# Early phase of a transformer block kernel recorded in the order in which its transfers are needed

## The chip, the cores and the metric

The kernel runs on one core of a Trainium2 chip. The metric is device time in microseconds (us) of one execution. 2% is the mark for calling one kernel faster than another. Engines: PE multiplies matrices, PEld is its weight loads, DVE and ACT work on vectors, POOL and SP in the early phase mostly issue transfers. A number such as L379 is a line of the kernel's source.

## The reference

```python
def reference(A_x, A_wqkv, A_wo, B_x, B_w_gate, B_w_up, B_w_down):   # x: 2048 x 1024, bf16
    h  = x + attention(layernorm(x) @ wqkv) @ wo     # 32 heads of 32; each position looks at
                                                     # 8 positions, 2 apart, itself and before
    n  = layernorm(h)
    return h + ((n @ w_gate) * (n @ w_up)) @ w_down  # F = 3584
```

(The attention is cut to a comment; B_x is not used.)

## The kernel before

The 2048 rows are cut into four chunks of 512. PE works through chunk after chunk; all other engines are to stay out of its way. Work of DVE and ACT that is not tied to a matmul is written as generators, from which a "background" draws pieces while the groups of matmuls are recorded: every group of PE (8 matmuls, 1.73 us) earns credit, every piece spends some. So it is the recording that fixes the order of each engine's instructions.

The projections to q, k and v are six blocks of weights (0 and 1 are q, 2 and 3 are k, 4 and 5 are v), each block four groups of eight matmuls. q, k and v go through memory, to turn the layout from features on partitions to (head, place) on partitions, and DVE does attention from there.

```python
def ln1(c):                                   # first normalization of chunk c, in the background
    xts = load_x(c, "x", nc.gpsimd)
    yield "later", 8.0 if c < 3 else 5.0
    ...
    def norm(t):
        ln = normalize(xts[t], mv4, rs4, t)
        nc.sync.dma_start_transpose(lnTs[c][:, :, bass.ts(t, 128)], ln[:])

load_x0(0); load_x0(1); load_w(2)             # first loads, in order, on the SP queue:
load_x0(2); load_w(2);  load_x0(3)            # x, x, block 0, x, block 1, x
...
def qkv(c, blocks, last=False):
    for b in blocks:
        for j in range(4):
            ps = psum.tile([128, TC], F32, tag="mm", ...)   # one of 8 banks
            mm_group(ps, wts["qkv", b], j, lnTs[c])         # PE: 8 matmuls
            evac_qkv(c, b * 4 + j, ps)                      # ACT copies, SP stores to memory
            bg.step(GROUP_US)
...
qkv(0, range(1, 6))          # all of q, k, v of chunk 0 (block 0's q is done in the start)
bg.add(ln1(3))
start_attention(0)           # loads q, k, v of chunk 0 through POOL, then DVE works
qkv(1, range(6))
start_attention(1)
qkv(2, range(6))
...
```

## Time and profile before

| kernel before | us |
|---|---|
| median of 3 runs | 813.73 (812.7 to 814.17) |
| span in the profile | 812.0 |
| PE busy | 795.3 |
| first matmul of full width (512 columns) | 20.23 |
| first product of attention on DVE | 67.82 |
| first matmul of the first output projection | 165.27 |
| first matmul of the last output projection | 491.47, after a wait of 4.88 |

The page's first two parts, for the kernel before. A row of the second part gives the busy tenths of an engine in 40 equal slices of the span, here 20.3 us each; PEclk is the granted clock of PE in tenths.

```profile
span 812.0 us, 9901 instructions
PE 795.3 (98%) x3700; PEld 410.6 (51%) x3769; DVE 551.8 (68%) x580; ACT 254.9 (31%) x562; POOL 171.8 (21%) x172
...
PE   7999999999999999999999997999999999999998
...
PEclk9999999999999999999999998999999999999999
```

PE is the bound: the row has three slices that are not full, the first, the 25th (near 490 us) and the last. The clock row has its one dent in the same 25th slice: there PE does not only stand, part of what it does afterwards runs at a lower clock (0.51 from 491.4 to 497.3 us). This wait of PE is thus paid twice, once as idle time and once as slow matmuls that look busy.

### The profile page before, as it was taken

Reading aid. Unit: us, or ns where it says so; the run is one execution under the profiler, and the core shown is the slowest. Engines: PE = TensorE matmul, PEld = TensorE weight load, DVE = VectorE, ACT = ScalarE, POOL = GpSimd, SP = SyncE. Lnnn points to the kernel's source line nnn. Section 1 sums busy time; section 2 is a strip of 40 time slices with the busy share of each in tenths; the row PEclk is TensorE's granted clock in tenths of the full one; section 3 lists DMA queues with packets and bytes.
Section 4 is the critical chain, followed back from the end, with each engine's and each line's share of the span. In section 5 each row is a group of like instructions: output and inputs, shape, how many; then the busy total and the mean of one; then the engine's idle time right before and its main releaser. Section 6 shows DMA issues by size and latency. Waiting matters only on the chain.

```text
span 812.0 us, 9901 instructions
## 1 busy us (share of the span) xinstructions
PE 795.3 (98%) x3700; PEld 410.6 (51%) x3769; DVE 551.8 (68%) x580; ACT 254.9 (31%) x562; POOL 171.8 (21%) x172
## 2 busy tenths in 40 slices
PE   7999999999999999999999997999999999999998
PEld 5444444444444444444444443466666666644445
DVE  4538999999899898999989945635646565311111
ACT  2554444314333310023333100245545555400000
POOL 3100000200001000002000001497878778100000
PEclk9999999999999999999999998999999999999999
DMA  9999564999855948848564596533323233465600
GB/s 310 317 254 235 123 192 105 260 281 253 289 161 189 316 117 277 281 132 288 182 199 145 136 312 141 129 99 84 103 54 104 55 102 90 152 219 182 187 27 27
DMA packets 194448, 144.32 MB, mean 178 GB/s; under 512 B 83424, under 2 KB 188000, under 8 KB 192352
## 3 DMA queue, kind: packets, MB, share of 16 engines
q1 hardware_dynamic: 189856, 118.51, 52.5%
q0 software_dynamic: 4544, 25.17, 8.9%
q8 instruction: 30, 0.49, 0.3%
q14 instruction: 18, 0.15, 0.1%
HBM read 114.29 MB, written 22.02 MB: 168 GB/s over the span
## 4 chain that ended last, share of the span: by engine, by line
PE 83%; issue 13%; DMA 3%; SPq 0%; POOL 0%; DVE 0%; ACT 0%; POOLq 0%
PE ps L343 19%; PE acc L524 18%; PE pg L343 7%; PE pu L343 7%; PE pz L575 6%; PE py L575 6%; PE px L575 6%; PE wo L466 5%; PE pv L575 3%; PE accl L514 3%; DMA od<-oD 1%; DMA x<-in_A_x_dram 1%; DMA oT<-od 1%; POOL oT L443 0%; SPq L226 0%
## 5 line engine op out<-in xcount | busy, mean ns | idle before, releaser
L343 PE MATMUL ps<-lnT,w_qkv 128*128 128x512 bf16 x721 | 158.4, 379 | 0.8
L343 PEld LDWEIGHTS <-w_qkv 128*128 128x128 bf16 x736 | 72.0, 98 | 86.6
L343 PE MATMUL pg<-lnT,w_wg 128*128 128x512 bf16 x439 | 105.0, 379 | 0.5
L343 PE MATMUL pu<-lnT,w_wu 128*128 128x512 bf16 x439 | 104.9, 379 | 0.4
L524 PE MATMUL acc<-w_wd,gs 128*128 128x512 bf16 x439 | 96.7, 379 | 0.5
L262 ACT CAST sg<-ps 128x512 bf16<-128x512 f32 x96 | 55.5, 586 | 65.3 <-PE ps L343 59.0
L506 DVE TENSOR_TENSOR h<-acc,h 128x512 bf16<-128x512 f32 x28 | 17.4, 682 | 81.8 <-PE acc L524 81.8
L428 DVE TENSOR_TENSOR pv<-vD,at 128x4096 bf16<-128x4096 bf16 x32 | 72.4, 2287 | 0.4
L388 DVE TENSOR_TENSOR prod<-qD,kD 128x4096 bf16<-128x4096 bf16 x32 | 72.3, 2285 | 0.0
L524 PEld LDWEIGHTS <-gs 128*128 128x128 bf16 x448 | 43.9, 98 | 52.8
L343 PEld LDWEIGHTS <-w_wg 128*128 128x128 bf16 x448 | 43.8, 98 | 52.9
L343 PEld LDWEIGHTS <-w_wu 128*128 128x128 bf16 x448 | 43.8, 98 | 52.9
L466 PE MATMUL wo<-w_wo,oT 128*128 128x512 bf16 x251 | 58.4, 392 | 5.1 <-DMA oT<-od 4.9
L491 ACT CAST gs<-pg 128x512 bf16<-128x512 f32 x56 | 32.8, 586 | 91.5 <-PE pg L343 88.1
L440 POOL DMA_DIRECT2D od<-oD x4 | 2.2, 544 | 251.0 <-DVE oD L438 153.5
L575 PE MATMUL px<-lnT,w_pair 128*128 128x512 bf16 x210 | 52.5, 380 | 0.9
L496 ACT CAST us<-pu 128x512 bf16<-128x512 f32 x56 | 32.8, 586 | 60.1 <-PE pu L343 54.4
L551 POOL TENSOR_TENSOR sw<-w_pair 128x512 fp32r<-128x512 bf16 x28 | 36.5, 1302 | 60.5 <-issue 32.2
L466 PEld LDWEIGHTS <-oT 128*128 128x128 bf16 x256 | 25.7, 101 | 37.4 <-DMA oT<-od 5.4
L178 ACT ACTIVATE rs<-mv,eps 128x1 f32<-128x1 f32 x32 | 9.4, 294 | 104.6 <-DVE mv L175 99.7
L553 POOL TENSOR_TENSOR sw<-w_pair 128x512 fp32r<-128x512 bf16 x28 | 36.9, 1318 | 0.0
L390 DVE TENSOR_TENSOR prod<-prod 128x4096 bf16<-128x4096 bf16 x16 | 36.6, 2289 | 0.3
(128 smaller groups left out, 1066.1 us busy)
## 6 DMA issues: line engine op xcount, KB each, us to landing
w_wd<-in_B_w_down_dram SPq DMA_DIRECT2D x32, 896.0 KB, 6.2
w_wg<-in_B_w_gate_dram SPq DMA_DIRECT2D x14, 1024.0 KB, 8.1
w_wu<-in_B_w_up_dram SPq DMA_DIRECT2D x14, 1024.0 KB, 6.0
w_wo<-in_A_wo_dram SPq DMA_DIRECT2D x8, 1024.0 KB, 6.9
w_pair<-in_B_w_gate_dram SPq DMA_DIRECT2D x14, 512.0 KB, 4.0
w_pair<-in_B_w_up_dram SPq DMA_DIRECT2D x14, 512.0 KB, 5.4
kd<-sg SPq DMA_DIRECT2D x32, 144.0 KB, 3.3
vd<-sg SPq DMA_DIRECT2D x32, 144.0 KB, 2.7
```

The lines of the kernel that those rows point to most:

```text
L262: nc.scalar.copy(sg[:, HB:HB + TC], ps[:])
L343: nc.tensor.matmul(ps[:], lhsT=wt[:, ko, bass.ts(j, 128)], rhs=rhs[:, ko, :], start=(ko == 0), stop=(ko == KO - 1))
L388: nc.vector.tensor_tensor(prod[:, j], qD[:], kD[:, :, o:o + SUB], ALU.mult)
L390: nc.vector.tensor_tensor(prod[:, :, 0:16], prod[:, :, 0:16], prod[:, :, 16:32], ALU.add)
L428: nc.vector.tensor_tensor(pv[:, j], vD[:, :, o:o + SUB], at[:, w, None, :].to_broadcast((128, DH, SUB)), ALU.mult)
L466: nc.tensor.matmul(ps[:], lhsT=oTs[c][:, kk, t, :], rhs=wts["wo", c, hf][:, kk, :], start=(kk == 0), stop=(kk == KO - 1))
L491: nc.scalar.copy(gs[:], pg[:])
L496: nc.scalar.copy(us[:], pu[:])
L524: nc.tensor.matmul(acc[t][:], lhsT=hT[f][:, bass.ts(t, 128)], rhs=wts["wd", c, hf, b][:, j, :], start=(f == 0), stop=(f == NF - 1))
L551: nc.gpsimd.tensor_tensor(sw[:, 0], a21, a22, ALU.add)
L553: nc.gpsimd.tensor_tensor(sw[:, 2], a11, a21, ALU.subtract)
L575: nc.tensor.matmul(ps[:], lhsT=lhs[:, ko, :], rhs=rhs[:, ko, :], start=(fresh and ko == 0), stop=(ko == 3), skip_group_check=not fresh)
```

## The change

The change records the early work in the order in which its data is needed. q and k of chunk 0 are followed by q and k of chunk 1, and only then by the two chunks' v; so attention, which begins with q and k, can begin sooner. The transposes of the "second normalization" (that of chunk 2) are held until the first q and k loads are out. And x's last tile of chunk 0 stands ahead of the second weight block, which waits for it. The first transposes now lie in two banks each. The x of chunks 1 to 3 is now loaded through SP's queue instead of POOL's, and the weights of later blocks are held back. The core of the diff (cut: the class that splits the normalization into statistics, normalization and transposes, the limits of `pump`, which loads the next weights, the wait for v, and renamings; the comments are mine):

```diff
     load_x0(0)
     load_x0(1)
-    load_w(2)
+    load_w0(0, 4)               # block 0 in two halves
     load_x0(2)
-    load_w(2)                   # block 1 in two halves
+    load_w0(4, 4)
     load_x0(3)
...
-        pts[t] = psum.tile([128, KO, 128], BF, tag="mm", name=f"pt{t}")
+        for hf in range(2):     # first transposes in two banks, so that DVE needn't follow ACT
+            pt = psum.tile([128, KO // 2, 128], BF, tag="mm", name=f"pt{t}_{hf}")
...
+    w1 = wpool.tile([128, KO, 512], BF, tag="w", name="w_qkv_1")
+    nc.gpsimd.tensor_copy(w1[:, 0, 0:1], x0[3][:, 0:1])   # block 1 waits for x's last tile
+    pump(2, w1)
+    xtiles[1] = load_x(1, "x", nc.sync)
+    pump(4)
+    xtiles[2] = load_x(2, "x", nc.sync)
...
-    qkv(0, range(1, 6))
-    bg.add(ln1(3))
+    qkv(0, range(1, 4))
+    load_qk(0)
+    bg.finish(rows2)
+    for t in range(4):
+        norm1[2].transpose(t)
+    xtiles[3] = load_x(3, "x", nc.sync)
+    pump(6)
+    bg.add(stats_gen(norm1[3]), bg.now + 6.0)
     start_attention(0)
-    qkv(1, range(6))
+    qkv(1, range(4))
+    qkv(0, range(4, 6))
+    load_v(0)
+    bg.add(norm_gen(norm1[3]), bg.now, first=True)
+    qkv(1, range(4, 6))
     start_attention(1)
```

More of the change, by code (lines that the diff above doesn't have):

```diff
@@ L154, with pump @@
     wts = {}
-    state = {"next": 0, "live": 0, "limit": pair_at}
-    def pump(eng=None):
+    state = {"next": 0, "live": 0, "limit": 1}
+    def pump(limit=None, wt=None):
+        state["limit"] = limit or state["limit"]
         while state["next"] < state["limit"] and state["live"] < 7:
             key, src, n = stream[state["next"]]
-            wt = wpool.tile([128, KO, 512], BF, tag="w", name="w_" + "_".join(map(str, key)))
-            (eng or nc.sync).dma_start(wt[:, 0:n, :], src)
+            if wt is None:
+                wt = wpool.tile([128, KO, 512], BF, tag="w", name="w_" + "_".join(map(str, key)))
+            nc.sync.dma_start(wt[:, 0:n, :], src)
             wts[key] = wt
+            wt = None
             state["next"] += 1
@@ L199, with __init__, stat, norm @@
     lnTs = {}
-    def ln1(c):
-        xts = load_x(c, "x", nc.gpsimd)
-        yield "later", 8.0 if c < 3 else 5.0
-        lnTs[c] = lnTp.tile([128, KO, TC], BF, tag="lnT", name=f"lnT1_{c}")
-        mv4, rs4 = ln_tiles(f"1_{c}")
-        def norm(t):
-            ln = normalize(xts[t], mv4, rs4, t)
-            nc.sync.dma_start_transpose(lnTs[c][:, :, bass.ts(t, 128)], ln[:])
+    xtiles = {}
+    class Norm1:
+        def __init__(self, c):
+            self.c = c
+            self.mv4, self.rs4 = ln_tiles(f"1_{c}")
+            self.lns = [None] * 4
+        def stat(self, t):
+            stats(xtiles[self.c][t], self.mv4, t)
+            rstd_of(self.mv4, self.rs4, t, t + 1)
+        def norm(self, t):
+            self.lns[t] = normalize(xtiles[self.c][t], self.mv4, self.rs4, t)
+        def transpose(self, t):
+            c = self.c
+            if c not in lnTs:
+                lnTs[c] = lnTp.tile([128, KO, TC], BF, tag="lnT", name=f"lnT1_{c}")
+            nc.sync.dma_start_transpose(lnTs[c][:, :, bass.ts(t, 128)], self.lns[t][:])
@@ L211, in ln1, with rows_gen, stats_gen @@
+    def rows_gen(n, transposed):
+        for t in range(5):
+            if t < 4:
+                n.stat(t)
+                yield 1.5
+            if t > 0:
+                n.norm(t - 1)
+                if transposed:
+                    n.transpose(t - 1)
+                yield 0.55
+    def stats_gen(n):
         for t in range(4):
-            stats(xts[t], mv4, t)
-            rstd_of(mv4, rs4, t, t + 1)
+            n.stat(t)
             yield 1.5
-            if t > 0:
-                norm(t - 1)
-                yield 0.55
@@ L218, in ln1, with norm_gen @@
-        norm(3)
-        yield 0.55
-    def load_w(parts=1):
-        key, src, n = stream[state["next"]]
-        wt = wpool.tile([128, KO, 512], BF, tag="w", name="w_" + "_".join(map(str, key)))
-        for q in range(parts):
-            nc.sync.dma_start(wt[:, bass.ts(q, KO // parts), :], src[:, bass.ts(q, KO // parts), :])
-        wts[key] = wt
-        state["next"] += 1
-        state["live"] += 1
+    def norm_gen(n):
+        for t in range(4):
+            n.norm(t)
+            n.transpose(t)
+            yield 0.55
@@ L231, with load_w0 @@
     x0 = [hp.tile([128, D], BF, tag="h", name=f"x0_{t}") for t in range(4)]
+    w0 = wpool.tile([128, KO, 512], BF, tag="w", name="w_qkv_0")
+    wts["qkv", 0] = w0
+    state["next"] += 1
+    state["live"] += 1
     def load_x0(t):
         nc.sync.dma_start(x0[t][:], x[bass.ds(t * 128, 128), :])
+    def load_w0(lo, n):
+        nc.sync.dma_start(w0[:, lo:lo + n, :], wqkv_v[:, lo:lo + n, 0:512])
     load_x0(0)
     load_x0(1)
-    load_w(2)
+    load_w0(0, 4)
     load_x0(2)
-    load_w(2)
+    load_w0(4, 4)
@@ L258 @@
         nc.tensor.matmul(wps[:], lhsT=warm[:, 0:128], rhs=warm[:], start=True, stop=True)
+    qkv_in = {}
     def evac_qkv(c, m, ps):
@@ L263, in evac_qkv @@
         hg = m % 8
+        if m >= 8:
+            nc.scalar.copy(sg[:, 0:HB], halo[:, m - 8, :])
+            if c + 1 < NCH:
+                nc.scalar.copy(halo[:, m - 8, :], ps[:, TC - HB:TC])
         if m < 8:
@@ L267, in evac_qkv @@
             return
-        nc.scalar.copy(sg[:, 0:HB], halo[:, m - 8, :])
-        if c + 1 < NCH:
-            nc.scalar.copy(halo[:, m - 8, :], ps[:, TC - HB:TC])
         dst = (kd, vd)[m // 8 - 1][c]
@@ L298, in first_transpose @@
     def first_transpose(t):
-        pts[t] = psum.tile([128, KO, 128], BF, tag="mm", name=f"pt{t}")
-        for kk in range(KO):
-            nc.tensor.transpose(pts[t][:, kk, :], lns[t][:, bass.ts(kk, 128)], ident[:])
-        nc.scalar.copy(lnTs[0][:, 0:4, bass.ts(t, 128)], pts[t][:, 0:4, :])
+        for hf in range(2):
+            pt = psum.tile([128, KO // 2, 128], BF, tag="mm", name=f"pt{t}_{hf}")
+            for kk in range(KO // 2):
+                nc.tensor.transpose(pt[:, kk, :], lns[t][:, bass.ts(4 * hf + kk, 128)], ident[:])
+            pts[t, hf] = pt
+        nc.scalar.copy(lnTs[0][:, 0:4, bass.ts(t, 128)], pts[t, 0][:])
     def first_copy(t):
-        nc.vector.tensor_copy(lnTs[0][:, 4:8, bass.ts(t, 128)], pts[t][:, 4:8, :])
+        nc.vector.tensor_copy(lnTs[0][:, 4:8, bass.ts(t, 128)], pts[t, 1][:])
     def first_mm(t, kos):
@@ L331 @@
     first_mm(3, range(8))
-    order_after_x0 = const.tile([128, 1], BF)
-    nc.gpsimd.tensor_copy(order_after_x0[:], x0[3][:, 0:1])
-    pump()
-    bg.add(ln1(1))
-    bg.add(ln1(2))
+    w1 = wpool.tile([128, KO, 512], BF, tag="w", name="w_qkv_1")
[4 more added lines that the diff above has]
+    xtiles[2] = load_x(2, "x", nc.sync)
+    norm1 = {c: Norm1(c) for c in (1, 2, 3)}
+    bg.add(rows_gen(norm1[1], True))
+    rows2 = rows_gen(norm1[2], False)
+    bg.add(rows2)
     for j in range(4):
@@ L356 @@
     oTs = {}
-    qkv_in = {}
     stored = set()
@@ L377, in attention @@
     def attention(c):
-        if c == 0:
-            load_qk(0)
-            load_v(0)
-            yield "later", 7.0
-        qD, kD, vD = qkv_in["q", c], qkv_in["k", c], qkv_in["v", c]
+        qD, kD = qkv_in["q", c], qkv_in["k", c]
         lg = att.tile([128, W, SUB], F32, tag="lg", name=f"lg{c}")
@@ L418, in attention @@
         prefetch_qk(c + 1)
+        while ("v", c) not in qkv_in:
+            yield "later", 1.0
+        vD = qkv_in["v", c]
         at = att.tile([128, W, SUB], BF, tag="at", name=f"at{c}")
@@ L620, in start_attention @@
         atts[c] = attention(c)
-        bg.add(atts[c], bg.now + (5.0 if c == 0 else 0.0))
-    qkv(0, range(1, 6))
-    bg.add(ln1(3))
-    start_attention(0)
-    qkv(1, range(6))
+        bg.add(atts[c], bg.now + (16.0 if c == 0 else 0.0))
+    qkv(0, range(1, 4))
+    load_qk(0)
+    bg.finish(rows2)
+    for t in range(4):
+        norm1[2].transpose(t)
+    xtiles[3] = load_x(3, "x", nc.sync)
+    pump(6)
+    bg.add(stats_gen(norm1[3]), bg.now + 6.0)
+    start_attention(0)
+    qkv(1, range(4))
[3 more added lines that the diff above has]
+    qkv(1, range(4, 6))
     start_attention(1)
+    pump(pair_at)
     qkv(2, range(6))
```

## The prediction

The row of GB/s is the DMA rate of the kernel before in slices of 1.5 us, from 0 to 60 us: 340 to 388 from 6.0 to 31.5 us. The 0.36 MB/us that the prediction works with is the mean of that stretch (360 GB/s). "The page" is the profile's, and "cold clock" stands for the granted clock of 0.51 in the second of its windows. 2.9 + 4.9 + 2.8 = 10.6 us off 813.7 is 803.1, and 0.9 for a small new wait makes 804.0.

> **What bounds the kernel now.** I read the page's first part first: PE is busy 795.3 of 812.0 us, so whatever the change does, it can win only what is in the remaining 16.7 us, about 2%. Next I read the waits of PE, to see where those microseconds are.
>
> ```profile
> PE wo L466 <- DMA oT<-od: 4.9, 1, 4.9
> PE pt L301 <- DVE ln L183: 2.4, 3, 1.3
> PE ps L310 <- ACT lnT L302: 1.4, 4, 0.7
> PE warm_ps L258 <- DVE warm L244: 1.2, 1, 1.2
> ```
>
> The columns are the sum, the number and the longest wait in us. There is one real stall, 4.9 us, of the output projection of the last chunk for its attention result. The rest lies in the start (the normalization of the first chunk, lines 301 and 310). To see what surrounds each, I cut PE into stretches.
>
> ```profile
> core 0: us, PE busy (x) PEld busy (x) DVE busy (x) ACT busy (x) POOL busy (x), PEclk, DMA share, GB/s
> 486.50:491.40 4.90, 0.09 (x1) 0.00 (x0) 1.97 (x4) 0.00 (x0) 2.94 (x4) 0.89 1.09 335
> 491.40:497.30 5.90, 5.83 (x15) 2.09 (x15) 0.69 (x1) 0.00 (x0) 0.00 (x0) 0.51 0.50 158
> 497.30:508.20 10.90, 10.85 (x51) 5.00 (x51) 9.58 (x18) 1.49 (x6) 0.00 (x0) 1.00 0.43 50
> 6.20:20.20 14.00, 10.23 (x161) 9.11 (x161) 6.59 (x15) 3.84 (x10) 4.79 (x9) 1.00 1.08 361
> ```
>
> The reader is to see that the stall has a tail that is called busy: for 5.9 us after it the granted clock is 0.51 and only 15 matmuls run. And from 6.2 to 20.2 us PE has 10.23 us of work in 14.0 us. The chain that ended last says what the two places hang on.
>
> ```profile
> 4.61 8.30 DMA x<-in_A_x_dram
> 476.19 9.13 DMA od<-oD
> 485.90 5.53 DMA oT<-od
> 491.47 12.04 PE wo L466 x42
> ```
>
> The start hangs on the fourth tile of x (issued at 4.61, landed at 12.9); the stall hangs on the end of the fourth attention, whose result goes to memory and back in about 15 us. So I read the timeline of DVE, which computes attention, and of the queues that feed it.
>
> ```profile
> 67.82 4.49 DVE L388 TENSOR_TENSOR prod<-qD,kD 128x4096 bf16<-128x4096 bf16 x2
> 450.98 2.28 DVE L438 TENSOR_TENSOR oD<-oD,pv 128x4096 bf16<-128x4096 bf16 x1
> 472.75 2.29 DVE L438 TENSOR_TENSOR oD<-oD,pv 128x4096 bf16<-128x4096 bf16 x1
> 23.99 11.76 SPq L265 DMA_DIRECT2D qd<-sg  x8
> 55.04 0.53 POOL L365 DMA_DIRECT2D kD<-kd  x1 [14.10 <-DMA kd<-sg]
> ```
>
> Attention begins at 67.8 us. DVE is above 80% in every fortieth of the span, and above 90% in most, from there to the end of attention at 475 us, so a later or earlier beginning is passed on. It begins late because the stores of q crawl (eight in 11.8 us, behind 5 MB of weights), so k is complete only at 55 us. Between 450.98 and 465.9 DVE works on the residual and normalization of the third chunk, and the last 9.1 us of attention come after that.
>
> [...] weight loads after the stall start 0.43 us apart until 497.3, and 49 matmuls take 10.74 us (219 ns each) elsewhere. [...] in slices of 1.5 us [...]:
>
> ```profile
> GB/s 0 188 242 329 367 373 360 359 352 349 348 360 378 373 388 368 361 350 349 353 340 295 186 222 235 301 336 245 169 459 329 290 267 230 147 234 127 207 307 332
> ```
>
> [...] x's first tile landed at 3.4, the first weight piece at 6.7, the third tile of x at 9.2, its fourth at 12.9, in the order of issue, but each about 1.5 to 2 us later than its own bytes at 0.36 MB/us would need. [...] each DVE copy out of the transposes starts 0.03 us after the ACT copy ended.
>
> **The change, part by part.** No matmul is added or removed; the built order has 6560 PE rows in both.
>
> 1. The first loads. Before, both blocks w0 and w1 (2 MB) stand among the x tiles and x's last tile is complete after 3 MB. After, w1 waits for x's last tile, which is thus complete after 2 MB. The bytes moved by the rate row above reach 2 MB at 8.4 us; with the lateness of about 1 us I put the landing at 9.3 us, not 12.9. The transposes are split over two banks, which takes away 0.6 to 0.7 us of DVE waiting per tile and lets ACT start after four transposes. Then PE becomes its own limit: from 6.2 us four times 0.62 (transposes) and 128 times 62.5 ns make 10.5 us, plus about 0.6 us for the first copies: 17.3 us in place of 20.2. **Gain 2.9 us** at the start.
>
> 2. w1 then is needed at 17.3. It is issued at about 9.9 into nearly empty rings. The first 1 MB of the kernel (issued at 0.76) took to 6.7 us, 5.9 us; so w1 lands at about 15.5 to 16. It holds, with 1.5 us to spare.
>
> 3. The order of blocks. Chunk 1 is needed after 12 groups instead of 20, at 17.3 + 12 x 1.73 = 38 us instead of 54.8. Its transposes stand in the queue behind the first q stores and one k store. With 5 MB from 10.3 us on (w1, x1, w2, w3, x2: 14 us at 0.36 MB/us plus start-up) the queue is free of its backlog at about 26 us, and the last transpose, behind the ninth store at 27.5, is issued at about 31 and landed at 35 to 36. It holds by about 2 us.
>
> 4. Attention. The last k store falls at 17.3 + 12 x 1.73 + 1 = 39 us; k lands 7 to 10 us after its issue at 43, so at 50 to 53. The third x load stands behind four transposes, so x3's statistics (7 us of DVE, which now stand before attention in DVE's order) end at about 57.5. Attention starts there: 10 us sooner. The four normalizations of x3 (4 x 0.55 us) move inside it, so its end gains about 8 us. It is filled in between PE groups at the same rate as before, so this carries through all four attentions. The built order confirms it: the last oD operation of attention 3 stood behind the last residual addition of the third chunk's projection, and now stands ahead of its first one. So it does not end at 475 but near 450, some 15 us of projection work earlier than the shift alone. Result back at about 470 (it also waits for the projection before, which reads the same buffer until 459), PE wants it at 484. **Gain: 4.9 us of stall and 2.8 us of cold clock** (63 matmuls in 16.78 us against 13.98 for those of the chunk before).
>
> The two gains are not independent: PE arriving 2.9 us earlier alone would only wait 2.9 us longer. With both, 2.9 + 4.9 + 2.8 = 10.6 us: 803.1. I add 0.9 for a small new wait early on (margins 1.5 and 2 us): **804.0 us**.
>
> **The rivals.** First: w1 comes late. The page gives 16.2 us as the middle time to landing of these 1 MB loads, which would put it at 26 and cost 8.7 us, eating nearly the whole gain: about 812. Against it: those 16.2 us were spent behind 3 MB of others, and w1 now is first. A wait of 1 to 2 us is quite possible: 805.
>
> Second: the transposes of chunk 1 come late. Before, the last was issued at 47.65, taking up to 3.2 us of the queue each. If they do so again, the last lands at 41 to 43 and PE waits 3 to 5 us, part of it with a cold clock after: 807 to 809. Against it: before, w4, w5, wo and the third x shared the engines then; they are held back now.
>
> Third: attention does not end sooner, since x3 or k comes late too. Then the stall only grows by what the start gained, and the time is 813. Against it stands the built order, which needs DVE only to keep up; DVE has over 15 us to spare at the end.
>
> Fourth: attention on DVE, running more behind its order, delays the normalization after the first projection, whose last transposes landed about 4 us ahead of PE. That would cost 1 to 3 us.
>
> **Range and chances.** With neither early wait, 803; with a small one, 805; with the second rival, up to 809. Below 801.5 there is nothing left to remove but the start itself. So 801.5 to 809 holds 8 in 10. Faster by over 2% means below 797.5, which asks for 16.2 us out of 16.7 us of PE's idle time and 2.8 us of cold clock: 2%. Slower by over 2%: 1%.
>
> **What would show it.** Right: no wait of PE for oT, no stretch with the clock at 0.5 after 480 us; the first full-width group at about 17.3; attention's first product at 55 to 60; x's fourth tile landing at 8.5 to 10. Wrong: PE waits for w_qkv near 17 us, or idles before chunk 1's first group near 38 us, or oT lands after PE has finished the block ahead of it.

## The result, and the profile after

The changed kernel takes **810.42 us** (median of 4 runs, 810.09 to 811.46) against 813.22 us for the kernel before in the same rounds (812.59 to 814.17). The ratio is 0.9967, with a 95% interval of 0.995 to 0.9984. The gain is real and 3 us, not 10.

The page's first two parts, for the kernel after:

```profile
span 808.9 us, 9878 instructions
PE 794.0 (98%) x3700; PEld 410.3 (51%) x3769; DVE 552.1 (68%) x580; ACT 254.3 (31%) x562; POOL 165.3 (20%) x160
...
PE   8889999999999999999999999999999999999998
...
PEclk9989999999999999999999999999999999999999
```

The hole near 490 us is gone, and two slices that were full, the second and third (20 to 61 us), no longer are; the clock row has its dent in the third, and no longer in the 25th. The waits of PE (sum, number, longest, in us) name the new one, and the windows show it and its tail (the numbers after PE, PEld, DVE, ACT and POOL are busy us and instructions):

```profile
PE ps L379 <- DMA lnT<-ln: 4.3, 1, 4.3
PE warm_ps L284 <- DVE warm L270: 1.2, 1, 1.2
PE ps L341 <- DMA w_qkv<-in_A_wqkv_dram: 1.1, 1, 1.1
```

```profile
core 0: us, PE busy (x) PEld busy (x) DVE busy (x) ACT busy (x) POOL busy (x), PEclk, DMA share, GB/s
38.22:42.48 4.26, 0.00 (x1) 0.03 (x2) 0.12 (x1) 0.94 (x4) 0.00 (x0) 0.89 0.86 271
42.48:48.08 5.60, 5.38 (x13) 1.97 (x15) 0.43 (x1) 0.59 (x1) 0.00 (x0) 0.50 1.34 200
488.00:504.50 16.50, 16.39 (x76) 7.50 (x77) 12.49 (x23) 1.49 (x6) 0.00 (x0) 1.00 0.65 161
```

PE stands 4.26 us for the transposed normalization of chunk 1 (tile lnT), and then works 5.6 us at half clock. The last line is the stretch that held the wait before: PE is full there, at a clock of 1.00. The chain that ended last names the transfer (start, duration, what):

```profile
28.20 3.17 DMA lnT<-ln
...
34.18 8.05 DMA lnT<-ln
42.23 0.25 issue
42.48 2.29 PE ps L379 x5
```

The first transpose on the chain took 3.17 us, the one that PE waits for 8.05. The timeline shows what else began then, and when the other things came that the prediction had put a time on (start, duration, engine, line, operation, output and input; in brackets the idle time before and its cause):

```profile
17.34 20.88 PE L379 MATMUL ps<-lnT,w_qkv 128*128 128x512 bf16 x94
34.44 0.70 POOL L399 DMA_DIRECT2D qD<-qd  x1 [24.38 <-DMA qd<-sg]
57.18 1.29 DVE L177 BATCH_NORM_STATS2 st<-x 128x6 f32<-128x512 bf16 x2 [14.28 <-DMA x<-in_A_x_dram]
62.81 4.45 DVE L419 TENSOR_TENSOR prod<-qD,kD 128x4096 bf16<-128x4096 bf16 x2
454.00 2.29 DVE L472 TENSOR_TENSOR oD<-oD,pv 128x4096 bf16<-128x4096 bf16 x1
```

The first full-width group comes at 17.34 (before 20.23), attention begins at 62.81 (before 67.82), and its last oD operation at 454.00 (before 472.75), as the new recording order wants it. And 0.26 us after the last transpose of chunk 1 was issued, the 1 MB load of q (qD) was, which took 8.0 us.

The balance is simple, because PE works on nothing but matmuls. From the first full-width group to the first matmul of the output projection PE needs 165.27 - 20.23 = 145.04 us without a stall. After the change it is 169.67 - 17.34 = 152.33, which is 7.29 us more: the wait of 4.26 and 3.03 us for the half clock. So the span moves by -2.89 (start) + 7.29 (new wait and clock) - 4.88 - 2.8 (old wait and clock) = -3.28; the spans differ by 3.1.

### The profile page after: what moved, and what is told of

It is laid out like the page before. It is cut to its first block, busy times and chain, and to the rows that moved or that the text cites. A ratio compares the mean times of both kernels' runs of the same rounds, so it can differ in the third digit from the quotient of the medians. Undisturbed runs are those within 1.5% of the kernel's fastest.

```text
span 808.9 us, 9878 instructions
## 1 busy us (share of the span) xinstructions
PE 794.0 (98%) x3700; PEld 410.3 (51%) x3769; DVE 552.1 (68%) x580; ACT 254.3 (31%) x562; POOL 165.3 (20%) x160
## 4 chain that ended last, share of the span: by engine, by line
PE 89%; DVE 7%; DMA 2%; issue 1%; ACT 0%; SPq 0%; DVEq 0%
PE ps L379 18%; PE acc L558 15%; PE pg L379 12%; PE pu L379 12%; PE wo L500 7%; PE pz L609 6%; PE py L609 6%; PE px L609 6%; PE pv L609 3%; PE accl L548 3%; DVE pv L462 2%; DMA lnT<-ln 1%; DVE pv L470 1%; PE ps L341 1%; DVE oD L472 1%
## 5 line engine op out<-in xcount | busy, mean ns | idle before, releaser
L379 PE MATMUL ps<-lnT,w_qkv 128*128 128x512 bf16 x721 | 161.3, 383 | 5.2 <-DMA lnT<-ln 4.3
L290 ACT CAST sg<-ps 128x512 bf16<-128x512 f32 x96 | 55.0, 587 | 68.9 <-PE ps L379 65.4
L500 PE MATMUL wo<-w_wo,oT 128*128 128x512 bf16 x251 | 55.6, 379 | 0.3
L530 ACT CAST us<-pu 128x512 bf16<-128x512 f32 x56 | 32.8, 587 | 57.5 <-PE pu L379 54.1
L181 ACT ACTIVATE rs<-mv,eps 128x1 f32<-128x1 f32 x32 | 9.5, 296 | 95.5 <-DVE mv L178 91.9
```

Source lines behind the costliest of these rows:

```text
L290: nc.scalar.copy(sg[:, HB:HB + TC], ps[:])
L379: nc.tensor.matmul(ps[:], lhsT=wt[:, ko, bass.ts(j, 128)], rhs=rhs[:, ko, :], start=(ko == 0), stop=(ko == KO - 1))
L500: nc.tensor.matmul(ps[:], lhsT=oTs[c][:, kk, t, :], rhs=wts["wo", c, hf][:, kk, :], start=(kk == 0), stop=(kk == KO - 1))
L530: nc.scalar.copy(us[:], pu[:])
```

## The experiments

Four calls were made, each on one chip, with runs of the kernel before on the same chip (medians 813.85, 814.28, 814.08 and 813.05). All results were correct. No kernel here reaches the 2% mark; a difference is called real where its 95% interval leaves out 1. The table has the balance of each run's profiled execution, which need not be the typical one (it is the fastest in e6_both, the slowest in e10_rstd_only); "lost early" is the column "between" less 145.04.

| run | first full-width group | output projection begins | between | lost early | wait for oT | median us |
|---|---|---|---|---|---|---|
| before | 20.23 | 165.27 | 145.04 | 0 | 4.9 | 813.73 |
| after | 17.34 | 169.67 | 152.33 | 7.29 | none | 810.42 |
| e1_hold_q | 16.84 | 169.06 | 152.22 | 7.18 | none | 810.37 |
| e2_x2_late | 17.42 | 175.38 | 157.96 | 12.92 | none | 815.55 |
| e3_warm | 17.48 | 168.03 | 150.55 | 5.51 | none | 809.05 |
| e4_loads_only | 17.94 | 170.06 | 152.12 | 7.08 | 3.7 and 4.4 | 818.26 |
| e5_stats_late | 16.83 | 169.81 | 152.98 | 7.94 | 3.8 | 814.59 |
| e6_both | 16.98 | 162.01 | 145.03 | 0 | 3.4 | 815.25 |
| e7_old_loads | 20.80 | 165.84 | 145.04 | 0 | none | 806.45 |
| e8_old_order | 17.26 | 167.26 | 150.00 | 4.96 | 3.8 and 3.6 | 815.31 |
| e9_hold_rstd | 16.57 | 166.13 | 149.56 | 4.52 | none | 807.76 |
| e10_rstd_only | 18.22 | 169.12 | 150.90 | 5.86 | none | 808.06 |
| e11_old_loads_both | 20.30 | 165.34 | 145.04 | 0 | none | 806.79 |
| e12_x3_first | 17.51 | 162.55 | 145.04 | 0 | none | 803.31 |

(In e4 and e8, and there alone, part of the lost time is a wait for oT at the first output projection itself.)

My theory after reading the two traces was that the q load slows the last transpose, and that this alone costs 7.3 us. (From 34.5 to 42.2 us in the kernel after, the profile counts 59.8% of the time of the 16 transfer engines for the packets of POOL's queue, and 42.5% for those of the other.) The rival was that the transposes are late by themselves: held up in the queue, by ACT and DVE, or by the bytes of x2's load. The two ask for different repairs.

### e1_hold_q: the q load waits for chunk 1's last transpose

```diff
     qkv(0, range(1, 4))
+    hold = const.tile([128, 1], BF)
+    nc.gpsimd.tensor_copy(hold[:], lnTs[1][:, 0, TC - 1:TC])   # POOL reads the last transpose's output
     load_qk(0)
```

> The changed kernel, with the load of q (1 MB, queued by POOL) held until the last of chunk 1's four transposes has landed. Theory A (that load, issued at 34.44 us, shares the DMA engines with the last transpose, issued at 34.18, and stretches it from 3.1-3.6 us to 8.1): the last transpose lands at about 37.7, PE's 4.26 us wait near 38 us and the cold clock after it (3.03 us) go, 810.4 becomes about 803.1, 0.990 of before. Rival B (the small-piece k stores slow it, or the transposes are simply issued too late): it still lands at 41 or later, the time stays at 809 to 811.

Measured: 810.37 us (809.79 to 810.86), ratio 0.9949 (0.9914 to 0.9984). The time did not move, although the cause of the wait was right: the last two transposes, issued at about 32.4 and 33.8 us, now land by 37.05 (when POOL's copy of the held column runs), in 3.2 to 3.6 us instead of 8.1, and the wait near 38 us is gone. But PE stands 20 us later, for as long. The waits of PE and the timeline of ACT in this run:

```profile
PE ps L379 <- ACT sg L290: 4.3, 1, 4.3
```

```profile
44.67 0.58 ACT L290 CAST sg<-ps 128x512 bf16<-128x512 f32 x1 [1.14 <-PE ps L379]
58.92 0.29 ACT L181 ACTIVATE rs<-mv,eps 128x1 f32<-128x1 f32 x1 [13.67 <-DVE mv L178]
```

ACT empties PE's banks (L290), and among these copies stand its two small operations for x3's statistics (L181). x3 lands only at about 57.3, so ACT idles 13.67 us, all copies behind it idle too, and PE, which has eight banks (the pool of the kernel), can run on for 8 groups of 1.73 us, 13.8 us: from the start of the last copy at 44.67 to 58.45, where it stopped, are 13.78. Copies whose banks had been full for up to 12.5 us stayed behind one operation that waited for x3, and the first of them began at 62.15, after that operation (58.92) and its like for two more tiles of x3. This **second limit** stood behind the first all along: in the kernel after, the wait at 38 us hid it.

### e2_x2_late: x2's loads behind chunk 1's transposes

```diff
     pump(4)
-    xtiles[2] = load_x(2, "x", nc.sync)
...
+    def rows2_late():
+        xtiles[2] = load_x(2, "x", nc.sync)
+        yield 0.05
+        yield from rows_gen(norm1[2], False)
```

> The changed kernel, with the loads of chunk 2's x moved in the SP queue from ahead of the first q stores to behind chunk 1's transposes; the q load is not touched. Theory A' (the first transpose left at 28.20 only since the queue ahead of it stood in waits for x2 landings; norms were ready from 20.9): the transposes leave 3 to 5 us sooner, all land by 36, no wait at 38 us, about 803 to 804. If instead the q load moves up with them (its q stores too leave sooner) and collides again, the last still takes 8 us but from an earlier start: a wait of 0 to 2 us, 803 to 806. Rival (the queue ahead is not what delays them): last transpose still leaves at 34 and the time stays at 810.

Measured: 815.55 us (814.45 to 816.47), ratio 1.0012 (0.9976 to 1.0048). The transposes left sooner (25.96 to 31.96 us) and still met the q load: the last took 5.3 us and landed at 37.3, just in time. But x2's own statistics now came late, and ACT stood for them as it did for x3's in e1: PE waited 5.5 us and 2.9 us for ACT. Moving a load back to make room moved the wait onto ACT. It is a second sight of that limit. As to the rival, it was half right: leaving 2.2 us sooner was also enough to clear the wait at 38 us, with the q load where it was. Lateness and stretching together made that wait, and taking away either one removes it.

### e3_warm: idle matmuls in the new wait

```diff
     start_attention(0)
+    wps1 = psum.tile([128, 512], F32, tag="mm", name="warm_ps1")
+    for i in range(18):
+        nc.tensor.matmul(wps1[:], lhsT=warm[:, 0:128], rhs=warm[:], start=True, stop=True)
     qkv(1, range(4))
```

> The changed kernel, with 18 idle matmuls (3.9 us warm) on a constant tile put before chunk 1's first group, inside PE's 4.26 us wait. It takes nothing from the wait, only keeps PE active in it. Theory (3.03 us of the loss is half clock after the wait): the wait's end stays at 42.5, no stretch at clock 0.5 follows, 810.4 becomes about 807.4, 0.993. Rival (slow matmuls after the wait are due to something else, such as DMA traffic into SBUF): they stay at 427 ns and the time stays at 810.

Measured: 809.05 us (808.83 to 810.97), ratio 0.994 (0.9897 to 0.9984). This measures the clock's share by itself. The idle matmuls filled 4.05 us from 38.20; after them the clock was 1.00 and no slow stretch followed, as the clock row of this run's page shows:

```profile
PEclk9999999999999999999999999999999999999999
```

Of the 3.03 us, 1.5 came back as a wait for ACT sg, the second limit again: 4.05 + 1.5 = 5.55 is what the table has as lost (5.51). So the slow stretch is a consequence of PE's idling and not of something in its data.

### e4_loads_only: the kernel before with only the new first loads

```diff
-    load_w(2)
+    load_w0(0, 4)
     load_x0(2)
-    load_w(2)
+    load_w0(4, 4)
     load_x0(3)
...   (two-bank transposes as in the change)
-    order_after_x0 = const.tile([128, 1], BF)
-    nc.gpsimd.tensor_copy(order_after_x0[:], x0[3][:, 0:1])
+    w1 = wpool.tile([128, KO, 512], BF, tag="w", name="w_qkv_1")
+    nc.gpsimd.tensor_copy(w1[:, 0, 0:1], x0[3][:, 0:1])
+    nc.sync.dma_start(w1[:], stream[1][1])
```

> The kernel before, with only the change's first loads (w0 in two halves, w1 held behind x's last tile) and the transposes split over two banks; order of blocks and all else as before. Theory of the prediction (a sooner start alone is waited off at oT, as attention on DVE does not end sooner by itself): first full-width group at 17.3 but the wait for oT grows from 4.9 towards 7.8, time 811 to 814, ratio about 1.00. Rival (attention moves up with the start): the wait stays 4.9 and the time is 810.3, ratio 0.996.

Measured: 818.26 us (812.52 to 819.96), ratio 1.0034 (0.9983 to 1.0085). The start gained 2.3 us in the profile and the rest lost more: waits for ACT halo (ACT's small copy of a chunk's last columns for the next chunk, 2.3), for weights (0.6) and for oT at both output projections (3.70 and 4.39), with attention starting at 71.07 in place of 67.82. A sooner PE by itself is worth nothing here, as the prediction had said of the two gains. That it costs time is not shown: the interval includes 1, and one execution took 812.52.

### e5_stats_late and e6_both: x3's statistics recorded later

e5_stats_late is the kernel after with the following edit, e6_both is e1_hold_q with it. It was to take the second limit away.

```diff
-    bg.add(stats_gen(norm1[3]), bg.now + 6.0)
+    bg.add(stats_gen(norm1[3]), bg.now + 16.0)
```

> The changed kernel, with the statistics of chunk 3 recorded 10 us of PE time later (ready at +16 in place of +6): VectorE's order hardly changes, ScalarE evicts some six more groups before it stands in the wait for those statistics (they wait for x3, landed at about 56). The q load is as in the changed kernel. Theory C (two limits in series: the late transpose at 38 us, then ScalarE stuck behind x3's statistics with all 8 PSUM banks full at 58.5 us; the first hides the second): the first limit stays, so 809.5 to 811, like the changed kernel. Rival (the second limit is the only true one): 803 to 806.

> The hold of the q load of e1_hold_q and the late statistics of e5_stats_late together. Theory C: both limits go; PE runs from 17 us to the end without a wait or a stretch at half clock, 810.4 less 4.3 and 3.0 is 803 (802.5 to 804.5), 0.988 of before. Rival (a third limit stands behind the two, the wait for oT for one): 805 to 810, with a wait that the trace names.

Measured: e5_stats_late 814.59 us (809.38 to 818.0), ratio 0.9972 (0.9907 to 1.0037); e6_both 815.25 us (806.64 to 816.6, 5 runs), ratio 0.9986 (0.9925 to 1.0046). In e5 the first wait stayed (5.0 us), as expected. e6_both has no wait at 38 or 58 us: nothing is lost early, so hold and statistics together do clear the first two limits. But both kernels had the old wait for oT again, 3.8 and 3.4 us. Pieces of background spend credit, and pieces recorded later leave it elsewhere: the last oD operation of attention 3 fell behind the third chunk's projection again, and its result left at 477.42 and 469.62 us, not at 456.58. The waits of PE and the timeline of DVE in e6_both (lines between left out):

```profile
PE wo L500 <- DMA oT<-od: 3.4, 1, 3.4
```

```profile
448.55 1.28 DVE L502 TENSOR_TENSOR h<-wo,h 128x512 bf16<-128x512 f32 x2
...
467.03 2.29 DVE L472 TENSOR_TENSOR oD<-oD,pv 128x4096 bf16<-128x4096 bf16 x1
```

L502 is the residual addition of the projection, and the last oD operation comes after it. This is a **third limit**: the end of attention holds its place in the recording by a narrow margin. The profiled execution of e6_both had a mean clock of 1.00 and took 806.64 us; its other four had 0.991 to 0.995 and took 813.42 to 816.6. The clock alone does not make that difference: a mean of 0.993 over 813.8 us stands for some 5.7 us (an estimate, 0.007 x 813.8; for the kernel after, 0.004 x 808.9 = 3.2 is close to its 3.03), and that execution took 9.05 us longer. So these four must have waited longer as well, which no trace shows.

### e7_old_loads: the change with the first loads of before

```diff
     load_x0(1)
-    load_w0(0, 4)
+    load_w(2)
     load_x0(2)
-    load_w0(4, 4)
+    load_w(2)
     load_x0(3)
...   (one-bank transposes as before)
-    w1 = wpool.tile([128, KO, 512], BF, tag="w", name="w_qkv_1")
-    nc.gpsimd.tensor_copy(w1[:, 0, 0:1], x0[3][:, 0:1])
-    pump(2, w1)
```

> The changed kernel, with the first loads and the one-bank transposes of the kernel before (w0 and w1 in quarters ahead of x's last tile). Theory C (start's gain of 2.9 us is given back at the waits that follow, since these hang on DMA and not on PE's start): first full-width group at 20.2, the waits of PE at 38 to 62 us are 2 to 4 us in place of 4.26 plus cold clock, time 809 to 811.5, the same as the changed kernel. Rival (gains add): 813.3.

Measured: **806.45 us** (806.21 to 806.86), ratio 0.9878 (0.9831 to 0.9926), 4 us faster than the whole change and below the 809 to 811.5 that were expected. (The first loads are in halves, not in quarters as the expectation has it.) PE starts 3.5 us later than in the kernel after (20.80) and stops nowhere any more (timeline of PE to 80 us, and of SP):

```profile
20.80 59.52 PE L375 MATMUL ps<-lnT,w_qkv 128*128 128x512 bf16 x269
```

```profile
31.05 2.65 SPq L225 DMA_TRANSPOSE lnT<-ln  x2
```

The collision is still there (the last transpose, issued at about 32.4 beside a q load at 32.7, took 6.9 us and landed at about 39.3), but PE wants it only at 20.80 + 20.76 = 41.6. So one part of the change undid the gain of another: the sooner start brought PE to data that had become later. With the new first loads x's loads for chunk 1 left at 10.51 instead of 6.79 and six q stores took 7.5 us of the queue instead of 4.0, and the last transpose landed at 42.2 instead of 39.3.

### e8_old_order: the old order of blocks, with the new loads

e6_both with v of chunk 0 ahead of q and k of chunk 1, as in the kernel before:

```diff
-    pump(4)
+    pump(6)
...
     start_attention(0)
-    qkv(1, range(4))
     qkv(0, range(4, 6))
     load_v(0)
-    bg.add(norm_gen(norm1[3]), bg.now, first=True)
-    qkv(1, range(4, 6))
+    bg.add(norm_gen(norm1[3]), bg.now + 12.0, first=True)
+    qkv(1, range(6))
```

> e6_both with the order of blocks of the kernel before (v of chunk 0 ahead of q and k of chunk 1, its weights loaded up front with the others); k of chunk 0 is still loaded after block 3. If the order of blocks is what frees the early phase: v's weights crowd the first 25 us, chunk 1's transposes and the k stores leave later, attention starts later (65 or more) and PE waits again at oT: 806 to 812. If it is not needed (only held transposes and early q and k loads are): 803 to 804.5, as e6_both.

Measured: 815.31 us (813.73 to 816.68), ratio 0.9986 (0.9935 to 1.0036). k's load left at 53.05, not 45.86 as in e6_both, attention began at 68.46, and both output projections waited for oT (7.4 us in all). So the old order brings a later attention and a new wait at the first output projection (3.8 us). About the gain at the end it says nothing, since e6_both, from which it differs, had lost that gain too (3.4 us against 3.6). The edit also moves the limit of the weight loads and the normalization of x3, so the order of blocks is not varied alone.

### e9_hold_rstd, e10_rstd_only, e11_old_loads_both: ACT's part of x3's statistics moved, nothing else

The third limit forbids moving the statistics, so only ACT's two small operations were gathered and put behind chunk 1's copies, which leaves DVE's order as it is. e9_hold_rstd is e1_hold_q with this edit, e10_rstd_only is the kernel after with it, e11_old_loads_both is e9_hold_rstd with the first loads of before.

```diff
 def stats_gen(n):
     for t in range(4):
-        n.stat(t)                                  # DVE statistics, then ACT's reciprocal root
+        stats(xtiles[n.c][t], n.mv4, t)            # DVE statistics alone
         yield 1.5
...
     qkv(1, range(4))
+    rstd_of(norm1[3].mv4, norm1[3].rs4, 0, 4)
     qkv(0, range(4, 6))
```

> The changed kernel with the q load held behind chunk 1's last transpose (as e1_hold_q) and, in place of e5's and e6's shift of the statistics, only the four pairs of ScalarE operations on x3's statistics gathered into one pair and put behind chunk 1's 16 q and k groups. VectorE's order stays word for word as in the changed kernel, so attention 3 ends ahead of the third chunk's projection again. Theory D (three limits in series: late transpose, ScalarE behind x3's statistics, and attention 3's last operations behind the projection, the last of which e5 and e6 brought back): no wait of PE after 17 us at all, clock 1.00, span about 801.5, time 802.5 to 804, little spread. Rival (the ScalarE path was not what held e1_hold_q): a wait near 58 us remains, 808 to 811.

> The changed kernel with only ScalarE's operations on x3's statistics moved as in e9; q is loaded as in the changed kernel. Theory D: the late transpose near 38 us stays (wait 4 to 5 us, then about 3 us of half clock), nothing behind it, so 809.5 to 811: the same as the changed kernel, though e1_hold_q alone does nothing either. Rival: 803 to 806.

> e9 with the first loads of the kernel before, as e7_old_loads. Theory D: e7 met none of the limits since its PE starts 2.9 us later and so arrives behind the transposes (39.3 against 41) and behind ScalarE's return (62); taking the limits away gains it nothing: 806 to 807, and e9 is 2.9 to 3.5 us faster, the sooner start at last paid out. Rival (the old first loads are better in themselves): at or below e9.

Measured: e9_hold_rstd 807.76 us (807.2 to 808.27), ratio 0.991 (0.9871 to 0.9949); e10_rstd_only 808.06 us (807.28 to 810.21), ratio 0.9911 (0.9864 to 0.9958); e11_old_loads_both 806.79 us (806.25 to 806.97), ratio 0.9897 (0.9858 to 0.9936).

e9_hold_rstd has no wait at 38 or 58 us and keeps the end in place (attention 3's result leaves at 453.04), and still loses 4.5 us: a **fourth limit**, near 108 us. The timelines of PE and ACT:

```profile
111.03 3.47 PE L379 MATMUL ps<-lnT,w_qkv 128*128 128x512 bf16 x8 [2.78 <-ACT sg L290]
```

```profile
94.47 0.59 ACT L290 CAST sg<-ps 128x512 bf16<-128x512 f32 x1 [0.83 <-PE ps L379]
109.45 1.06 ACT L439 ACTIVATE lg<-lg 128x1024 f32<-128x1024 f32 x1 [14.39 <-DVE lg L438]
110.41 3.98 ACT L290 CAST sg<-ps 128x512 bf16<-128x512 f32 x8
```

It is the second limit's pattern again: ACT's next instruction is the Exp of attention 0, which needs a subtraction on DVE that ended at 109.4; behind the Exp stand eight copies, and PE has filled its eight banks: it stopped at 108.25, again 13.78 us after the start of ACT's last copy (94.47). That Exp is late because attention 0 began at 62.77, behind the statistics of x3, whose load stood in the queue behind four held transposes and landed at 57.1. e10_rstd_only says that without the hold the wait at 39 us stays (4.0 us; the profile names a k store, which landed at 42.97, as did the last transpose), and that then PE comes late enough to miss the fourth limit. This is its slowest execution (810.21); the other three took 807.28 to 808.2, below the range that was expected, at the same clock (0.998), and no trace shows what they waited for. e11_old_loads_both says that with the old loads PE comes late enough to miss all four, so that neither hold nor gathering adds anything to e7_old_loads.

### e12_x3_first: x3's load ahead of the held transposes

e9_hold_rstd with one move, which was to take the fourth limit at its root:

```diff
     bg.finish(rows2)
+    xtiles[3] = load_x(3, "x", nc.sync)
     for t in range(4):
         norm1[2].transpose(t)
-    xtiles[3] = load_x(3, "x", nc.sync)
     pump(6)
```

> Edit: the run with both the hold and the gathered reciprocal roots (e9_hold_rstd, 807.76 us), with the four loads of x's fourth chunk recorded ahead of the four held transposes of the second normalization. Theory: in that run ACT stood from 94.5 to 109.45 us because its next instruction, attention 0's Exp, needed a subtraction that DVE ended only at 109.4, since attention 0 began at 62.77, behind the statistics of a chunk whose loads were issued at 48.1 to 51.6 us, behind the held transposes, and landed at 57.1; with the PSUM banks full PE then stood 2.78 us. The loads now go out from about 39.1 us and land by about 49; the statistics end by about 55 and attention 0 begins at 55 to 57.5 us, the subtraction ends by about 104 and the wait of PE near 108 us is gone or below 0.5 us. The transposes leave about 3.5 us later and are needed only near 100 us. Time: 807.8 less 2.8 and some clock effect, about 804.5 us (803.5 to 805.5), so better than the runs with the old first loads (806.45). Rival 1: the statistics moved ahead stand on DVE in front of something that ACT or PE needs sooner, or ACT's order has another wait behind: attention 0 begins sooner but a wait of PE of 1 us or more for ACT sg appears elsewhere, and the time stays at 806.5 to 808. Rival 2: the wider traffic between 39 and 49 us delays kD's load or the weights of chunk 2 (a wait for w_qkv): 806 to 809.

Measured: **803.31 us** (803.0 to 803.63), ratio 0.9874 (0.9858 to 0.9891), 1.2 us better than expected and below the range that was given. The clock is 1.00 in all four runs. The timelines of PE, DVE and ACT:

```profile
17.51 112.83 PE L379 MATMUL ps<-lnT,w_qkv 128*128 128x512 bf16 x511
```

```profile
58.60 4.49 DVE L419 TENSOR_TENSOR prod<-qD,kD 128x4096 bf16<-128x4096 bf16 x2 [5.53 <-DMA kD<-kd]
```

```profile
105.32 1.06 ACT L439 ACTIVATE lg<-lg 128x1024 f32<-128x1024 f32 x1 [9.33 <-DVE lg L438]
```

x3 landed at 47.4 instead of 57.1; attention began at 58.60 (a little later than the 55 to 57.5 expected, as it now waits for k and no longer for x3), the Exp came 4.1 us sooner, and PE runs through from 17.51 to the end of the window without a stop. Between the first full-width group and the output projection lie 145.04 us. The held transposes now took 15.4 us to issue, which nothing waits for. The range was missed because it put nothing on the slow clock after e9_hold_rstd's wait beyond some tenths. In the profiled executions 4.52 us were lost there, 2.78 of wait and, as what is left, 1.74 of clock; with PE's start 0.94 us later, 807.20 - 4.52 + 0.94 = 803.62, and e12_x3_first's took 803.60.

This kernel does what the change set out to do: against the kernel before of the same rounds (813.05, 812.32 to 815.13) it is 9.7 us faster. It has little in hand: the last transpose of chunk 1 had landed by 37.96 (the hold's copy), and PE wanted it at 17.51 + 20.76 = 38.27.

## Why the prediction was wrong

**What held.** Step 1: the fourth tile of x landed at 9.9 (predicted 9.3) and the first full-width group came at 17.34 (17.3). That this fits so well is partly luck: PE's work from 6.2 us was 9.63 us and not 10.5, and it stood 1.05 us for the second half of w0, which the sum had not. (Two of its readings are off without harm: the matmuls of "219 ns" are of 216, since the pieces of 10.74 us begin 10.79 apart and the 50th record is missing; and the landings are 0.5 to 1.4 us later than its rate row gives, an estimate, not 1.5 to 2. Step 1 used 1.) Step 2: w1 was issued at 10.09 (the DMA rate from 9.0 to 10.5 was 7 GB/s) and landed near 15.1 (15.5 to 16), so the first rival did not come; nor did the third and the fourth, as PE has no wait for oT and none behind the first projection. Step 4, in its outcome: no wait for oT, no slow clock after 480 us, both worth the 4.88 and 2.8 us that were counted, and attention's last oD operation at 454 (near 450). In its working it was less good: attention began at 62.81, not at 57.5. The prediction knew that x3's load stands behind four transposes, but gave that queue too little: the loads were issued at 50.2 and took 7 us. At the end this did not matter, since the new recording order, and not the earlier beginning, frees the last oD operation: e6_both began attention at 62.56, as soon as the kernel after, and its last oD operation, recorded behind the projection, ended late. Which part of the change set that order was not isolated. The late beginning did matter near 108 us, as e9_hold_rstd and e12_x3_first show.

**What failed: step 3**, "the last transpose ... is issued at about 31 and landed at 35 to 36. It holds by about 2 us". It was issued at 34.18, 3 us late (the queue was free of its backlog at 28.2, not 26), and took 8.05 us, so it landed at 42.2, and PE stood 4.26 us: the sign of being wrong that the prediction had named, PE idle before chunk 1's first group near 38 us. The prediction gave a transpose 4 to 5 us whatever flew beside it. In e1_hold_q the last two took 3.2 to 3.6 us with the q load held back: the load of 1 MB on the other queue had more than doubled the last. At 3.6 us the late issue would still have been in time (37.8 against 38.22, an estimate); e2_x2_late shows that an earlier issue is in time too. The prediction did not ask what happens when the two queues meet, as the change made them; how the transfers of two queues are served was not shown, but what it costs was to be seen even in the kernel before: its early transposes took 3.1 to 3.5 us with no load from POOL in flight and 4.7 to 7.8 beside one.

**What was mis-sized.** The second rival named this wait and its length (3 to 5 us), for another cause (w4, w5, wo and x3, which indeed were held back), and then gave 807 to 809. Its sum counted the clock only in part. Wait and clock came to 7.29 us, as much as the pair at the end, 7.68 us, for which the prediction had counted both. 803.1 + 7.3 = 810.4 is the measured time.

**What was missing.** No rival asked what stands behind the first wait. e1_hold_q removed that wait and won nothing, because ACT stands in front of PE's banks with instructions that wait for x3 (13.67 us), and the copies recorded behind them stood too. Behind that stood the Exp of attention 0. These limits are shown one by one: hold alone (810.37), hold and gathered roots (807.76), and x3 first as well (803.31). The last is where the prediction's own sum without a new wait stood (803.1): the gains were all there, and the changed kernel gave 7.3 us of them back between 38 and 48 us.

**What stays open.** Whether PE's clock falls after a wait of 3 us differs from execution to execution as far as the mean clocks tell (e9_hold_rstd: 0.998 twice, 1.00 twice), and nothing that was run controls that. In the profiled executions the clock fell at a wait of 2.78 us (e9_hold_rstd) and stayed at 1.00 after one of 3.4 us (e6_both). It was 0.50 for 3.4 us in e9_hold_rstd (110.9 to 114.3) and in e10_rstd_only (44.4 to 47.8, from 1.3 us after the wait had ended), both worked out from the mean clock of windows, and for 6.8 us in the kernel before (490.3 to 497.2) and the kernel after (41.5 to 48.3), where the return came 5.7 and 5.8 us after work had begun again. Runs of kernels in which PE waits for a transfer spread by up to 10 us (e6_both 806.64 to 816.6; the kernel before 811.4 to 821.2 over all rounds), while e7_old_loads, e11_old_loads_both and e12_x3_first, which have no such wait after 21 us, spread by less than 1. The clock does not make the whole of this spread: the kernel before took 812.62 us at a mean clock of 0.995 and 818.53 at 0.996, and of e9_hold_rstd's executions the two at 1.00 (807.42, 808.1) were no faster than the two at 0.998 (807.2, 808.27). So the waits differ between executions as well; each kernel has a trace of one execution only.

## What to carry to other kernels

Before moving PE's work forward, list for each input not only when it is issued but what else is in flight with it: here a small transpose beside a 1 MB load on another queue took 8.05 us in place of 3.2 to 3.6. Then look for instructions of the engine that empties PE's banks which wait for late data, since PE outran them here only by its eight groups (13.78 us); they formed limits one behind the other, and removing the first alone showed nothing (e1_hold_q). As an estimate from these traces, count a wait of PE of 3 to 5 us as about 1.5 to 1.7 times its length, for the slow clock after it: 2.78 us cost 4.52, 4.02 cost 5.86, 4.26 cost 7.29, 4.88 cost 7.68. The 3.4 us of e6_both cost nothing more in the one execution that was profiled.
